# Attention in front of an expert layer: queries' transfers, grouping of weights and block sums rearranged

## The chip, the cores and the metric

The kernel runs on one core of a Trainium2 chip. The metric is device time in microseconds (us) of one execution; three timed runs of the kernel before gave 818.00, 818.36 and 817.81, median 818.0. The core's engines are TensorE (PE; PEld is its weight load), VectorE (DVE), ScalarE (ACT), GpSimd (POOL) and SyncE (SP), which here issues nearly all transfers. Each engine works through its own list of instructions in order and waits on semaphores for the others.

## The reference

```python
batch, n_heads, seq, head_dim = (4, 8, 576, 64)
scores = scale * np.matmul(q, k.transpose(0, 1, 3, 2))
log_f = np.log(np.clip(f, 0.0001, 1.0))
cum = np.cumsum(log_f, axis=-1)
decay = cum[:, :, :, None] - cum[:, :, None, :]
scores = np.where(causal, -1000000000.0, scores + decay)
scores = scores - np.max(scores, axis=-1, keepdims=True)
attn = np.exp(scores)
attn = attn / (np.sum(attn, axis=-1, keepdims=True) + 1e-09)
return np.matmul(attn, v).astype(np.float32)
```

The result, reshaped to 2304 tokens of 512 features, goes through `((x @ w1) * (x @ w2)) @ w3 @ w_out` and then through a layer of eight experts, where every token takes the expert with the largest gate. The change touches attention alone.

## The kernel before

Two heads make a pair; there are 16 pairs, numbered n from 0 to 15. 576 positions are five blocks of 128 (the last has 64). What is done for a pair is cut into stages with short names; `START` gives each stage a planned time in its pair, and `order` in `attention` sorts all stages of all pairs by `START + SHIFT + 9.8 n`. The instructions are issued in that order, and each engine then keeps it. The numbers of `START` set the order only: an instruction runs as soon as its engine comes to it and what it needs is there.

A pair goes through these stages:

- `lk`, `lq`, `lv`: SP loads transposed keys, queries, and values (288, 288 and 320 KB). `ck`: two small transfers bring the decay terms (CK).
- `kh`, `qh`: ScalarE rounds keys and queries to fp32r; `kl`, `ql`: VectorE makes the remainders. `qd` (`last_queries`): SP copies the last 64 queries of both heads from `qh` into the diagonal of a tile QD, two transfers.
- `X1`, `X3`, `X2` (with block 0) and `XL` (the last 64 queries of both heads, with QD): TensorE makes rounded scores; `m1`, `m3`, `m2`, `m0`, `mL`: VectorE takes their row maxima into M.
- `Tm`: TensorE turns the maxima (a product with the identity) into a corner of a bank; `tc`: ScalarE copies them; `mv`: SP spreads them into the rows MR.
- `GA` to `GD`: TensorE makes the exact scores, keys as rows, in four groups of columns, three terms each; `HA` to `HD` add decay and maxima as a fourth term; `eA` to `eD`: ScalarE takes the exponential of a group into the tile PT. `BANKS` says which block's columns stand in which group, `BLOCK` where a block stands in PT.
- `a0` to `a4`: POOL zeroes the upper triangle of a diagonal block (affine select). `s1` to `s3`: POOL adds blocks 0 to 3 into `ac`.
- `p0`, `p1`, `p3`: TensorE multiplies the weights with the values; `su` (`sums`): products with a column of ones sum `ac`, the first columns of block 0, and block 4 over the keys. `xa`, `sa`: ScalarE copies the result and the sums; `zs`: SP stores the sums; `rl` to `rs` invert them once per batch.

Three banks of 1024 columns (pool `pss`) go round among the X and G stages, so a G or X product waits until the exponential or the maxima three allocations before have read theirs.

In one round TensorE runs GB, GA of pair n-2, X1 of pair n, GC, X3, X2, GD, XL of pair n, Tm of pair n-1, then p0 to p3 and su of pair n-3.

Woven in is work for later products: SP loads pieces of weights (`c0`, 512 KB), ScalarE and VectorE take them apart (`c1` on ScalarE; `c2`, `c3`, `c4` on VectorE), ScalarE rounds them (`c5`, line 505), POOL makes the residual (`c6`, line 507). In eight rounds SP also issues a zero fill of `xs` (`cr`, 771 KB), and in some the broadcast of reciprocals (`xl`, tile rb).

Of the kernel before, what the change touches and what calls it, by code (L numbers as in the profile page):

```python
# [28 lines left out]
P = 128  # L29
# [11 lines left out]
EARLY = 12  # L41
LOADS = 5

BLOCK = [(0, 192), (128, 768), (256, 1216), (384, 0), (512, 1536)]
WIDTH = 1600

BANKS = {"A": [(3, 384, S), (0, 0, 288)], "B": [(0, 288, S)], "C": [(1, 128, S)], "D": [(2, 256, S), (4, 512, S)]}

PERIOD = 9.8
START = {  # L50
# [7 lines left out]
}  # L58
SHIFT = {
    (1, "lk"): -9.0, (1, "lq"): -9.2, (2, "lk"): 1.0, (2, "lq"): 1.0, (0, "Tm"): -3.7, (0, "tc"): -3.65, (0, "mv"): -3.7,  # L60
    (15, "xa"): -3.4, (15, "sa"): -3.4, (15, "zs"): -5.9, (15, "rl"): -5.9,
}

FILL = {(0, "XL"): 8, (1, "XL"): 5}

AFTER = {
    "K4_13": 4.4, "K4_14": 4.43, "K0_15": 15.6, "K0_16": 15.61, "K0_17": 15.62, "inputs": 13.6, "scores": 13.8,
# [11 lines left out]
def attention(nc, tc, ident, xT, rz, xs, wc, q, k, v, f):  # L79
# [7 lines left out]
    with (  # L87
# [136 lines left out]
        def pairwise(*products):  # L224

            for x in products:
                for h in range(2):
                    out, a, b, start, stop = x
                    PE.matmul(out(h), a(HALF[h]), b(HALF[h]), start=start, stop=stop)  # L229
# [40 lines left out]
        def turn(s):  # L270
            n = s["n"]
            if n == B * NP - 1:
                x = pss.tile([P, 1024], F32, name=f"t_{n}", tag="s")[:, 896:]
            else:
                x = st[n + 1 if n else n]["x", 4][:, 896:]
            s["t"] = x[0:64, :P]
            PE.matmul(s["t"], Ms[s["n"] % 2], ident, start=True, stop=True)

# [8 lines left out]
        def weights(s, g, last):  # L287

            n = s["n"]
            if not last:  # L290
                s["g", g] = pss.tile([P, 1024], F32, name=f"g{g}_{n}", tag="s")
            ps = s["g", g]
            terms = [(s["kh"], s["qh"]), (s["kl"], s["qh"]), (s["kh"], s["ql"])] if not last else [(CKs[n % 3], MRs[n % 2])]
            (j, q0, q1), *more = BANKS[g]
            if j == 2:
                more, s["tail"] = [], s.get("tail", []) + terms
            for i, (a, b) in enumerate(terms):
                at = 0
                for x, (j, q0, q1) in enumerate([BANKS[g][0], *more]):
                    kc, c = slice(P * j, P * j + P), slice(at, at + q1 - q0)  # L300
                    out = lambda h: ps[:, 512 * h + c.start:512 * h + c.stop]
                    pairwise((out, lambda r: a[r, kc], lambda r: b[r, q0:q1], not last and i == x == 0, last and x == len(more)))
                    at = c.stop
            if j == 2 and last:
                tail = lambda e: lambda h: ps[64 * e:64 * e + 64, 512 * h + at:512 * h + at + SL]
                pairwise((tail(1), lambda r: z[r, :SL], lambda r: z[r, :SL], True, True))
                for i, (a, b) in enumerate(s["tail"]):
                    pairwise((tail(0), lambda r: a[r, 512:S], lambda r: b[r, 512:S], i == 0, i == len(s["tail"]) - 1))

        def expo(s, g):  # L310
            w = sum(q1 - q0 for _, q0, q1 in BANKS[g])
# [35 lines left out]

        def sums(s):

            acc = s["ac"]  # L350
            for half, c, src, start, stop in (
                (1, 0, lambda h: acc[:, h, 160:448], True, False), (0, 0, lambda h: place(s, 0, h, 0, P), True, True),
                (0, P, lambda h: acc[:, h, 0:160], True, True), (1, 224, lambda h: place(s, 4, h, 512, S), False, True),
            ):
                for h in range(2):
                    r = 64 * h + 32 * half
                    x = src(h)
                    PE.matmul(s["v"][r:r + 32, c:c + x.shape[1]], ones, x, start=start, stop=stop, tile_position=(0, r))

# [2 lines left out]
            A.activation(out=xT[:, pr, S * b:S * b + S], in_=s["v"][:, 384:960], func=ACTF.Copy)  # L362

        def keep_sums(s):
            A.activation(out=tl(s, "zs", (288,)), in_=s["v"][:, 0:288], func=ACTF.Copy)

        def store_sums(s):
            b, pr = divmod(s["n"], NP)
            SP.dma_start(out=zd[pr, :, S * b:S * b + S].rearrange("h (i c) -> h i c", i=2), in_=s["zs"][0:P:32])

        def invert(s, step, late=False):

# [947 lines left out]
```

## Time and profile before

| | us |
|---|---|
| median of three timed runs | 818.0 |
| the profiled execution | 816.79 |
| its span | 815.2 |
| TensorE busy in the span | 780.6 (96%) |
| VectorE, POOL, ScalarE busy | 453.3, 320.7, 281.0 |

The span runs from the first instruction to the last. Attention takes about its first 208 us. In the page's forty slices (20.4 us each) TensorE is 0.8 or 0.9 busy in the first ten, 0.9 after that:

```profile
PE   8899888899999999999999999999999999999995
DVE  7897877785689960441333223046577836445520
POOL 5568877799100040131023021014355443445521
PEclk9899998999999999999999999999999999999999
DMA  2546566534454310100010010034576656557460
```

Each digit is a tenth of the slice (PEclk: of TensorE's full clock). A busy TensorE can still be at the lower clock. A timeline row reads: start, duration, engine, line, operation, output and inputs, shapes, count; in brackets the idle time before it and who ended it. A wait for several semaphores is put down to the one that came last by the profile.

### The profile page before, as it was taken

Reading aid. Unit: us, or ns where it says so; the run is one execution under the profiler, and the core shown is the slowest. Engines: PE = TensorE matmul, PEld = TensorE weight load, DVE = VectorE, ACT = ScalarE, POOL = GpSimd, SP = SyncE. Lnnn points to the kernel's source line nnn. Section 1 sums busy time; section 2 is a strip of 40 time slices with the busy share of each in tenths; the row PEclk is TensorE's granted clock in tenths of the full one; section 3 lists DMA queues with packets and bytes.
Section 4 is the critical chain, followed back from the end, with each engine's and each line's share of the span. In section 5 each row is a group of like instructions: output and inputs, shape, how many; then the busy total and the mean of one; then the engine's idle time right before and its main releaser. Section 6 shows DMA issues by size and latency. Waiting matters only on the chain.

```text
span 815.2 us, 13776 instructions
## 1 busy us (share of the span) xinstructions
PE 780.6 (96%) x5166; PEld 657.5 (81%) x5167; DVE 453.3 (56%) x987; ACT 281.0 (34%) x542; POOL 320.7 (39%) x339
## 2 busy tenths in 40 slices
PE   8899888899999999999999999999999999999995
PEld 4777766686788887888788788898898999999983
DVE  7897877785689960441333223046577836445520
ACT  3555554565447522221221221222222222322221
POOL 5568877799100040131023021014355443445521
PEclk9899998999999999999999999999999999999999
DMA  2546566534454310100010010034576656557460
GB/s 94 157 147 195 166 219 195 178 127 138 128 186 155 129 41 27 52 26 28 27 39 20 8 52 0 1 117 143 191 234 196 195 191 196 169 189 225 138 265 29
DMA packets 40211, 102.12 MB, mean 125 GB/s; under 512 B 8610, under 2 KB 9314, under 8 KB 39888
## 3 DMA queue, kind: packets, MB, share of 16 engines
q1 hardware_dynamic: 36960, 91.46, 35.3%
q0 software_dynamic: 3184, 9.77, 3.2%
q8 instruction: 41, 0.67, 0.3%
q14 instruction: 26, 0.21, 0.1%
HBM read 84.47 MB, written 16.51 MB: 124 GB/s over the span
## 4 chain that ended last, share of the span: by engine, by line
PE 77%; DMA 7%; POOL 6%; DVE 3%; issue 3%; SPq 2%; ACT 1%; POOLq 0%; DVEq 0%; ACTq 0%
PE a L592 4%; PE b L592 4%; PE y L594 4%; PE y L592 4%; PE a L594 4%; PE b L594 4%; PE y L593 4%; PE a L593 4%; PE b L593 4%; PE h L592 3%; PE h L594 3%; PE h L593 3%; DMA QD<-qh 3%; DMA out<-ot,id 3%; PE v L342 3%
## 5 line engine op out<-in xcount | busy, mean ns | idle before, releaser
L622 DVE TENSOR_TENSOR ga<-b,ga 128x512 f32<-128x512 f32 (+1 forms) x40 | 25.4, 636 | 144.0 <-PE b L594 143.3
L753 POOL DMA_INDIRECT xs<-xr,pos x18 | 19.0, 1055 | 172.7 <-DVE pos L747 126.6
L264 DVE CUSTOM_DVE_ANT_0 junk<-x,tri 128x256 f32<-128x256 f32 (+3 forms) x128 | 62.7, 490 | 16.9 <-PE x L229 9.6
L592 PE MATMUL h<-gh,ah 128*128 128x320 f32 (+4 forms) x224 | 67.2, 300 | 0.0
L593 PE MATMUL h<-gl,ah 128*128 128x320 f32 (+4 forms) x224 | 66.9, 299 | 0.0
L594 PE MATMUL h<-gh,al 128*128 128x320 f32 (+4 forms) x224 | 66.9, 299 | 0.0
L321 POOL TENSOR_SCALAR_AFFINE_SELECT PT<-PT 128x256 f32<-128x256 f32 (+1 forms) x80 | 55.9, 732 | 15.9 <-ACT PT L315 12.4
L592 PE MATMUL b<-xh,w2h 128*128 128x512 f32 (+1 forms) x160 | 59.9, 375 | 0.0
L592 PE MATMUL a<-xh,w1h 128*128 128x512 f32 (+1 forms) x160 | 59.8, 374 | 0.0
L594 PE MATMUL a<-xh,w1l 128*128 128x512 f32 (+1 forms) x160 | 58.9, 368 | 0.0
L594 PE MATMUL b<-xh,w2l 128*128 128x512 f32 (+1 forms) x160 | 58.9, 368 | 0.0
L593 PE MATMUL a<-xl,w1h 128*128 128x512 f32 (+1 forms) x160 | 58.8, 368 | 0.0
L593 PE MATMUL b<-xl,w2h 128*128 128x512 f32 (+1 forms) x160 | 58.8, 368 | 0.0
L342 PE MATMUL v<-PT,vr 128*64 128x448 f32 (+4 forms) x384 | 56.9, 436 | 1.5 <-POOL ac L333 1.5
L592 PE MATMUL y<-raw,gh 128*128 128x512 f32 x144 | 56.9, 395 | 0.0
L594 PE MATMUL y<-raw,gl 128*128 128x512 f32 x144 | 56.2, 390 | 0.0
L593 PE MATMUL y<-raw,gh 128*128 128x512 f32 x144 | 56.0, 389 | 0.0
L585 POOL TENSOR_SCALAR bh<-rb 128x1024 fp32r<-128x1024 f32 x28 | 37.6, 1344 | 44.1 <-DMA rb<-e 39.8
L624 ACT ACTIVATE gh<-ga 128x512 fp32r<-128x512 f32 (+1 forms) x40 | 23.5, 588 | 88.9 <-DVE ga L622 88.9
L342 PEld LDWEIGHTS v<-PT,vr 128*64 128x64 f32 x384 | 41.7, 151 | 15.4 <-issue 4.2
L1046 DVE SCALAR_TENSOR_TENSOR hl<-h,hh 128x320 fp32r<-128x320 f32 (+4 forms) x56 | 25.5, 463 | 46.9 <-ACT hh L1045 46.2
L608 POOL TENSOR_TENSOR xT<-xT,rz 128x512 f32<-128x512 f32 (+1 forms) x16 | 19.8, 1235 | 77.0 <-DMA rz<-rz 77.0
(619 smaller groups left out, 2156.0 us busy)
## 6 DMA issues: line engine op xcount, KB each, us to landing
ra<-e SPq DMA_DIRECT2D x28, 512.0 KB
rb<-e SPq DMA_DIRECT2D x28, 512.0 KB
w<-w3t SPq DMA_DIRECT2D x16, 512.0 KB
xs<-zero SPq DMA_DIRECT2D x8, 771.0 KB
vr<-v SPq DMA_DIRECT2D x16, 320.0 KB
kr<-k SPq DMA_DIRECT2D x16, 288.0 KB
qr<-q SPq DMA_DIRECT2D x16, 288.0 KB
wo<-wo SPq DMA_DIRECT2D x8, 512.0 KB
```

The costliest lines, as they stand in the source:

```text
L264: V.tensor_tensor_reduce(out=junk[:, :w], in0=s["x", i][:, 512 * h:512 * h + w] if i < 4 else s["x", i][:, 224:224 + S], in1=tri[:, 640 - ...
L321: G.affine_select(out=t, in_=t, pattern=[[0, 2], [1, w]], compare_op=ALU.is_ge, fill=0.0, base=0, channel_multiplier=-1,)
L342: PE.matmul(s["v"][HALF[h], 384 + q0:384 + q1], s["vr"][:, j, HALF[h]], place(s, j, h, q0, q1), start=(j == 0), stop=(j == 4 or q1 == P),)
L585: G.tensor_scalar(out=hi, in0=src, scalar1=1.0, scalar2=1.0, op0=ALU.mult, op1=ALU.mult)
L592: PE.matmul(ps, ah, bh, start=start and i == 0, stop=False)
L593: PE.matmul(ps, ah, bl, start=False, stop=False)
L594: PE.matmul(ps, al, bh, start=False, stop=stop and i == last)
L608: G.tensor_tensor(out=xv, in0=xv, in1=d, op=ALU.mult)
L622: V.tensor_tensor(out=ga[:, :w], in0=pb[:, :w], in1=ga[:, :w], op=ALU.mult)
L624: A.activation(out=gh[:, f, :w], in_=ga[:, :w], func=ACTF.Copy)
L753: return G.indirect_dma_start(out=xs[:, :], out_offset=bass.IndirectOffsetOnAxis(ap=pos[:, c:c + 1], axis=0), in_=rows[c], in_offset=None, ...
L1046: V.scalar_tensor_tensor(out=hl[:, f, :w], in0=ps[:, :w], scalar=0.0, in1=hh[:, f, :w].bitcast(F32), op0=ALU.max, op1=ALU.subtract)
```

## The change

Six things, in the order of the diff:

- Groups of columns: A is 288 columns of block 0, B its other 288, C block 1 with block 4 (448 and 64), D block 2 with block 3 (320 and 192); before A had block 3 with the first 288 of block 0, B 288, C block 1, D block 2 and the tail (block 4) on half the rows. A now comes before B. Products of block 4 have all 128 rows, and the zero product for the unused rows is gone.
- `qd` stands before `c0`, so ahead of the weights' load, the zero fill and the broadcasts.
- `c5` stands between `eB` and `eC` instead of after `tc`; `c6` and the selects move earlier, with a4 before a2 and a3.
- `s3` is gone: POOL adds blocks 0 to 2 only, and TensorE sums block 3's 192 columns in `sums`. The sums are split at column 384 instead of 288; they are copied in two pieces and stored with two transfers.
- Pair 1's turn (`Tm`, `tc`, `mv`) comes 4.4 of the plan's units sooner; it then uses its own pair's bank.
- Four fill products stand after X1 of pair 1.

```diff
-BLOCK = [(0, 192), (128, 768), (256, 1216), (384, 0), (512, 1536)]
+BLOCK = [(0, 0), (128, 576), (256, 1088), (384, 1408), (512, 1024)]
-BANKS = {"A": [(3, 384, S), (0, 0, 288)], "B": [(0, 288, S)], "C": [(1, 128, S)], "D": [(2, 256, S), (4, 512, S)]}
+BANKS = {"A": [(0, 0, 288)], "B": [(0, 288, S)], "C": [(1, 128, S), (4, 512, S)], "D": [(2, 256, S), (3, 384, S)]}
+HALVES = (0, 384, S)
...
-    "lk": -18.7, "lq": -18.2, "ck": -15.75, "kh": -14.1, "qh": -13.2, "c0": -12.6, "qd": -10.7,
+    "lk": -18.7, "lq": -18.2, "ck": -15.75, "kh": -14.1, "qh": -13.2, "qd": -12.5, "c0": -12.4,
...
+    (1, "Tm"): -4.45, (1, "tc"): -4.45, (1, "mv"): -4.4,
...
-FILL = {(0, "XL"): 8, (1, "XL"): 5}
+FILL = {(0, "XL"): 8, (1, "X1"): 4, (1, "XL"): 5}
...
-                x = st[n + 1 if n else n]["x", 4][:, 896:]
+                x = st[n + 1 if n > 1 else n]["x", 4][:, 896:]
...
-            (j, q0, q1), *more = BANKS[g]
-            if j == 2:
-                more, s["tail"] = [], s.get("tail", []) + terms
...
-            if j == 2 and last:
-                tail = lambda e: lambda h: ps[64 * e:64 * e + 64, 512 * h + at:512 * h + at + SL]
-                pairwise((tail(1), lambda r: z[r, :SL], lambda r: z[r, :SL], True, True))
-                for i, (a, b) in enumerate(s["tail"]):
-                    pairwise((tail(0), lambda r: a[r, 512:S], lambda r: b[r, 512:S], i == 0, i == len(s["tail"]) - 1))
...
-            acc = s["ac"]
-            for half, c, src, start, stop in (
-                (1, 0, lambda h: acc[:, h, 160:448], True, False), (0, 0, lambda h: place(s, 0, h, 0, P), True, True),
-                (0, P, lambda h: acc[:, h, 0:160], True, True), (1, 224, lambda h: place(s, 4, h, 512, S), False, True),
+            acc = lambda q0, q1: lambda h: s["ac"][:, h, q0 - P:q1 - P]
+            mid = HALVES[1]
+            for half, q0, src, start, stop in (
+                (1, mid, acc(mid, S), True, False), (0, 0, lambda h: place(s, 0, h, 0, P), True, True),
+                (1, 384, lambda h: place(s, 3, h, 384, S), False, False), (0, P, acc(P, mid), True, True),
+                (1, 512, lambda h: place(s, 4, h, 512, S), False, True),
             ):
                 for h in range(2):
-                    r = 64 * h + 32 * half
+                    r, c = 64 * half + 32 * h, q0 - HALVES[half]
...
-            A.activation(out=tl(s, "zs", (288,)), in_=s["v"][:, 0:288], func=ACTF.Copy)
+            zs, n = tl(s, "zs", (HALVES[1],)), S - HALVES[1]
+            A.activation(out=zs[:, :n], in_=s["v"][:, :n], func=ACTF.Copy)
+            A.activation(out=zs[0:64, n:], in_=s["v"][0:64, n:HALVES[1]], func=ACTF.Copy)
...
-            SP.dma_start(out=zd[pr, :, S * b:S * b + S].rearrange("h (i c) -> h i c", i=2), in_=s["zs"][0:P:32])
+            for i, (q0, q1) in enumerate(zip(HALVES, HALVES[1:])):
+                SP.dma_start(out=zd[pr, :, S * b + q0:S * b + q1], in_=s["zs"][64 * i:64 * i + 64:32, :q1 - q0])
```

The rest of `START` is told by what stands in each engine's list. On SP, in the round of pair 6, before (MR: maxima of pair 4; zd: sums; wo: a piece of weights; xs: zero fill; kr, qr: the loads for pair 7):

```order
L195 DMA MR_111<-mt_868 2x1x64
L369 DMA zd<-zs_842 2x2x288
L489 DMA wo_895<-wo 128x512
L404 DMA xs<-zero 128x3x514
L195 DMA QD_120<-qh_887 64x64 x2
L200 DMA vr_948<-v 128x640
L200 DMA kr_967<-k 128x576
L200 DMA qr_971<-q 128x576
L209 DMA CK_109<-EKd 2x576 x2
```

And now:

```order
L198 DMA MR_111<-mt_870 2x1x64
L369 DMA zd<-zs_851 2x384
L369 DMA zd<-zs_851 2x192
L198 DMA QD_120<-qh_889 64x64 x2
L489 DMA wo_904<-wo 128x512
L404 DMA xs<-zero 128x3x514
L203 DMA vr_943<-v 128x640
L203 DMA kr_969<-k 128x576
L203 DMA qr_975<-q 128x576
L212 DMA CK_109<-EKd 2x576 x2
```

QD went ahead of the weights and the zero fill; the store of the sums became two.

On ScalarE, a round in the middle, before (PT: exponentials; zs: sums; mt: turned maxima; cw: rounded weights):

```order
L315 ACTIVATE PT_941<-gB_914 128x2x288
L315 ACTIVATE PT_941<-gA_927 128x2x480
L315 ACTIVATE PT_941<-gC_958 128x2x448
L362 ACTIVATE xT<-v_870 128x576
L365 ACTIVATE zs_999<-v_870 128x288
L315 ACTIVATE PT_941<-gD_991 128x2x384
L280 ACTIVATE mt_1025<-xl_1016 9x128
L505 ACTIVATE cw<-wo1u 128x512
L215 ACTIVATE kh_116<-kr_967 128x576
L215 ACTIVATE qh_1044<-qr_971 128x576
L496 ACTIVATE w01u<-w_739 128x512
```

And now:

```order
L310 ACTIVATE PT_938<-gA_921 128x2x288
L310 ACTIVATE PT_938<-gB_931 128x2x288
L505 ACTIVATE cw<-wo1u 128x512
L310 ACTIVATE PT_938<-gC_953 128x2x512
L359 ACTIVATE xT<-v_872 128x576
L363 ACTIVATE zs_1009<-v_872 128x192
L364 ACTIVATE zs_1009<-v_872 64x192
L310 ACTIVATE PT_938<-gD_995 128x2x512
L283 ACTIVATE mt_1028<-xl_1019 9x128
L218 ACTIVATE kh_116<-kr_969 128x576
L218 ACTIVATE qh_1047<-qr_975 128x576
L496 ACTIVATE w01u<-w_747 128x512
```

The rounding of the piece wo1 went from behind the turned maxima to between the second and the third exponential.

On POOL, the same round, before (ac: the running sum; cw: the residual of the piece), from the residual on:

```order
L507 TENSOR_TENSOR cw<-wo1u,cw 128x512
L321 AFFINE_SELECT PT_941<-PT_941 128x2x128 x4
L321 AFFINE_SELECT PT_941<-PT_941 128x2x64
L333 TENSOR_TENSOR ac_1120<-PT_941 128x896
L333 TENSOR_TENSOR ac_1120<-ac_1120,PT_941 128x2x320
L333 TENSOR_TENSOR ac_1120<-ac_1120,PT_941 128x2x192
```

And now:

```order
L507 TENSOR_TENSOR cw<-wo1u,cw 128x512
L316 AFFINE_SELECT PT_938<-PT_938 128x2x128 x2
L316 AFFINE_SELECT PT_938<-PT_938 128x2x64
L316 AFFINE_SELECT PT_938<-PT_938 128x2x128 x2
L328 TENSOR_TENSOR ac_1104<-PT_938 128x896
L328 TENSOR_TENSOR ac_1104<-ac_1104,PT_938 128x2x320
```

The third add is gone and the select of the last block comes third. The order of residual, selects and adds stays; what the residual waits for stands earlier on ScalarE.

## Rows read from the trace of the kernel before

**Rows 1.** Windows of core 0: us, busy time (count) of each engine, clock, DMA share, GB/s

```profile
29.80:36.60 6.80, 6.00 (x44) 5.84 (x44) 4.48 (x9) 2.68 (x4) 4.21 (x5) 0.50 0.69 218
200.00:210.00 10.00, 8.24 (x67) 5.53 (x61) 2.93 (x5) 2.40 (x7) 7.51 (x7) 1.00 0.16 55
210.00:220.00 10.00, 10.00 (x46) 8.26 (x45) 9.70 (x18) 5.87 (x12) 0.00 (x0) 1.00 0.56 165
```

**Rows 2.** Waits of TensorE, 0 to 210 us: total, times, longest

```profile
PE xl L256 <- DMA QD<-qh: 10.4, 5, 3.3
PE xl L256 <- DVE M L264: 2.8, 3, 1.7
PE gB L229 <- DMA MR<-mt: 1.9, 1, 1.9
...
PE v L358 <- POOL ac L333: 1.8, 1, 1.8
PE v L342 <- POOL ac L333: 1.5, 2, 0.9
```

**Rows 3.** Timeline, first product of XL, pairs 3, 4, 5, 6 and 15

```profile
37.83 0.40 PE L256 MATMUL xl<-kh,QD 128*128 128x288 f32 x1
49.55 0.40 PE L256 MATMUL xl<-kh,QD 128*128 128x288 f32 x1
59.32 0.40 PE L256 MATMUL xl<-kh,QD 128*128 128x288 f32 x1
70.98 0.58 PE L256 MATMUL xl<-kh,QD 128*128 128x288 f32 x1 [1.73 <-DVE M L264]
...
179.24 0.40 PE L256 MATMUL xl<-kh,QD 128*128 128x288 f32 x1
```

**Rows 4.** Timeline of SP: issues of weights and QD in two rounds

```profile
62.71 0.36 SPq L489 DMA_DIRECT2D wo<-wo  x1
...
63.70 2.50 SPq L195 DMA_DIRECT2D QD<-qh  x2
...
75.12 0.36 SPq L489 DMA_DIRECT2D w<-w3t  x1
...
149.80 0.40 SPq L489 DMA_DIRECT2D w<-w3t  x1
```

**Rows 5.** Windows at the end of two bursts; last two columns DMA share, GB/s

```profile
71.00:72.00 1.00, 1.00 (x4) 0.93 (x4) 0.00 (x0) 0.00 (x0) 0.38 (x1) 0.50 0.45 166
...
159.50:160.00 0.50, 0.50 (x4) 0.38 (x2) 0.35 (x1) 0.50 (x2) 0.00 (x0) 0.51 0.23 74
```

**Rows 6.** Timeline of POOL and VectorE: kl alone, and in the round from 37.83

```profile
15.26 0.75 DVE L222 TENSOR_TENSOR kl<-kr,kh 128x576 fp32r<-128x576 f32 x1
...
39.47 2.11 POOL L333 TENSOR_TENSOR ac<-PT 128x896 f32<-128x896 f32 x1
40.08 2.11 DVE L222 TENSOR_TENSOR kl<-kr,kh 128x576 fp32r<-128x576 f32 x1
42.11 2.11 DVE L222 TENSOR_TENSOR ql<-qr,qh 128x576 fp32r<-128x576 f32 x1
44.14 1.24 DVE L498 TENSOR_SCALAR wo0u<-wo0u 128x512 int32<-128x512 int32 x1
```

**Rows 7.** The same two engines in the round from 59.32

```profile
61.51 1.29 POOL L507 TENSOR_TENSOR cw<-w00u,cw 128x512 fp32r<-128x512 f32 x1
61.94 1.48 DVE L222 TENSOR_TENSOR kl<-kr,kh 128x576 fp32r<-128x576 f32 x1
66.58 2.12 POOL L333 TENSOR_TENSOR ac<-PT 128x896 f32<-128x896 f32 x1
```

**Rows 8.** Groups by form, 0 to 200: count, busy us, mean ns, idle before

```profile
L333 POOL TENSOR_TENSOR ac<-ac,PT 128x384 f32<-128x384 f32 x15 | 16.2, 1079 | 1.2
L315 ACT ACTIVATE PT<-gC 128x896 f32<-128x896 f32 x16 | 14.7, 919 | 2.2 <-PE gC L229 1.3
L215 ACT ACTIVATE qh<-qr 128x576 fp32r<-128x576 f32 x16 | 10.7, 670 | 0.9 <-DMA qr<-q 0.9
L358 PE MATMUL v<-ac,ones 128*32 128x160 f32 x60 | 6.6, 299 | 0.0
```

More of the change, by code (lines that the diff above doesn't have):

```diff
@@ L293, in weights @@
             terms = [(s["kh"], s["qh"]), (s["kl"], s["qh"]), (s["kh"], s["ql"])] if not last else [(CKs[n % 3], MRs[n % 2])]
-            (j, q0, q1), *more = BANKS[g]
-            if j == 2:
-                more, s["tail"] = [], s.get("tail", []) + terms
             for i, (a, b) in enumerate(terms):
                 at = 0
-                for x, (j, q0, q1) in enumerate([BANKS[g][0], *more]):
+                for x, (j, q0, q1) in enumerate(BANKS[g]):
                     kc, c = slice(P * j, P * j + P), slice(at, at + q1 - q0)
                     out = lambda h: ps[:, 512 * h + c.start:512 * h + c.stop]
-                    pairwise((out, lambda r: a[r, kc], lambda r: b[r, q0:q1], not last and i == x == 0, last and x == len(more)))
+                    pairwise((out, lambda r: a[r, kc], lambda r: b[r, q0:q1], not last and i == x == 0, last and x == len(BANKS[g]) - 1))
                     at = c.stop
-            if j == 2 and last:
-                tail = lambda e: lambda h: ps[64 * e:64 * e + 64, 512 * h + at:512 * h + at + SL]
-                pairwise((tail(1), lambda r: z[r, :SL], lambda r: z[r, :SL], True, True))
-                for i, (a, b) in enumerate(s["tail"]):
-                    pairwise((tail(0), lambda r: a[r, 512:S], lambda r: b[r, 512:S], i == 0, i == len(s["tail"]) - 1))
         def expo(s, g):
```

8 rows, old and new, of the table START are left out of this document.

## The prediction

> **What bounds the kernel now.** I read the page's busy line and windows first, then TensorE's waits, then the timeline of the places named there. From 210 us on TensorE is busy throughout; in the ten before that for 8.24 [rows 1]. So the change, which touches only attention, has to win its time before 208 us, and what it wins is then carried through some 600 us of full TensorE.
>
> Attention runs in rounds, one pair of heads per round; I count them by the start of XL (the score product of the last 64 queries): 49.55 for pair 4, 59.32 for pair 5, 179.24 for pair 15 [rows 3]. The round from pair 4 to 5 takes 9.77. The eleven rounds from pair 4 to 15 take 129.69, 11.79 each: two microseconds a round are stalls. The largest wait by name is XL's for QD, 10.4 in five waits; the second name, VectorE's M, may hide more of the same, as a wait for several semaphores is put down to the last. At the end of attention TensorE waits 1.5 + 1.8 = 3.3 for POOL's running sum, and early once 1.9 for MR [rows 2].
>
> Why QD is late: SP issues 0.5 MB of weights at 62.71, the 771 KB zero fill, and only then QD at 63.70 [rows 4]. XL of that pair starts at 70.98 [rows 3], when the traffic is nearly over: from 71 to 72 the DMA engines are 0.45 busy [rows 5]. SP gets to the next weights at 75.12 [rows 4], since MR stands before them and waits for the turn behind XL. The DMA engines are thus idle from about 71.5 to 75.
>
> **The change part by part.**
>
> *QD ahead of weights and zero fill.* XL's wait for QD goes. What is late next? QD waits for qh, qh for the load of its queries, and that load is the last of the previous round's burst. Behind QD on SP now stand the weights, the zero fill, the broadcasts and the loads of values, keys and queries. So a loop of transfers closes: weights issued, burst lands, qh, QD issued, next weights. The burst runs from 62.71 to about 71.5 in traffic [rows 4, 5]; its last piece lands, I estimate, 9.2 after the weights' issue (8.8 to 9.6). Less 0.35 for the QD no longer in it (an estimate: 32 KB in short rows), plus 0.7 for qh [rows 8], plus 1.1 for two QD issues (the two before took 2.50 with the queue full, an issue alone about 0.5) and 0.1 of waking: 10.8 to 11.1 a round. A round with the broadcast of reciprocals issues its weights at 149.80 and ends its traffic at about 160, 10.2 later [rows 4, 5]; the same sum gives 12.2, and as I see traffic only to half a microsecond I take 12.4. Three rounds are of that kind. The second store of the sums adds one SP issue of 0.5, beside TensorE.
>
> *POOL's third add goes, its order moves.* The add of 128x384 costs 1.08 a round [rows 8]. At the end of attention POOL was the last to finish; there its 3.3 of waits go, and I take 3.0 (1 to 4), because MR of the last pair is next.
>
> In the rounds the move is worth less, perhaps nothing. POOL and VectorE take turns: in the round from 37.83 the first add runs from 39.47 to 41.58; kl starts at 40.08 and takes 2.11, where alone it took 0.75; ql takes 2.11 and the first weight step 1.24 [rows 6]. That round, in which TensorE waits for no transfer, took 49.55 - 37.83 = 11.72 [rows 3]. From the next round on ScalarE's weight rounding stands after the turn, and POOL's residual behind it, at 61.51; the add then falls at 66.58, kl takes only 1.48 [rows 7], and the round from 49.55 takes 9.77. The change puts the rounding between the second and the third exponential. POOL's residual is then early, the selects follow the exponentials, and the add starts some 2 us after D, where the round of 37.83 had it.
>
> So I price the new round by that one. From XL at 37.83: kl ends at 42.19, ql at 44.22 [rows 6]. The first weight step takes 0.62 rather than 1.24, as the third add beside it is gone; two more of 0.7: 46.2. Rounding 0.65 (a 128x576 copy is 0.67 [rows 8]): it is now in front of the third exponential, and while it waits for VectorE's last step, that exponential, the copies of the finished pair and the fourth are queued behind it, and D's product for its bank. Third exponential 0.92 [rows 8], 1.0 with 1024 instead of 896 elements; D's product 1.0 (as for the fourth block 320 and 192 columns a head in four terms); XL at 48.9. That is 11.1, and 0.2 more, since D's exponential grows from 768 to 1024 elements and moves the add. Round: 11.3. Bounds: 9.8, if the add falls beside the maxima as now, and 12.6, if POOL's residual of 1.29 [rows 7] blocks VectorE as well.
>
> [...]
>
> *TensorE's own work.* The tail products of D (ten of 64 columns) become eight in C; 192 columns move from A to D; sums gets 192 more columns a head in fp32. The nearest row, 160 columns of sums, is 0.30 an instruction, several side by side [rows 8]: I put sums at +0.2 and the tail at -0.3, so -0.1 a round (-0.4 to +0.3), hidden where the round is 11.3. The second copy of the sums on ScalarE adds some 0.3, hidden in its idle time before the fourth exponential.
>
> *Second pair's turn sooner.* In the third round B's product waits 1.9 for MR [rows 2], and TensorE's granted clock is 0.50 from 29.8 to 36.6 [rows 1], the lower of its two levels. Now the turn stands before the third pair's scores. MR is issued some microseconds sooner, but behind weights and values (0.8 MB, at the burst's 2.2 MB in 8.8 some 3.3 us), so I let it land 1.9 sooner than now, and the third pair's keys and queries, which moved behind it, only about when they are wanted. XL of pair 3 then 2.2 sooner, and the next round without the third add 0.8 shorter: -3.0 up to pair 4 (-5 if the half clock goes too, -1 if the transfers behind MR decide). The four fill products stand where TensorE waits for the first turn anyway and cost nothing; without that cover some 0.9.
>
> *Sum.* Eight rounds of 11.3 and three of 12.4 are 127.6, against 129.7: -2.1. With -3.0 before and -3.0 behind: -8.1. The profiled execution took 816.79 (span 815.2 and 1.6 around it), 1.2 below the median of 818.0; 816.8 - 8.1 = 808.7, or 809.9 beside the median. I predict 810.
>
> **Rivals.**
>
> A, *the add falls beside the maxima all the same*: then only the loop of transfers counts. For it: POOL worked that way in most rounds [rows 7]; against it: nothing in the new order holds POOL back. Five rounds of 10.9, three of 12.4, three without zero fill of 9.8 are 121; with late landings 124. So -6 to -9 in the middle and -6 outside: about 805. If the loop were shorter too, eleven rounds of 9.7 would give -23, some 790; I see no reason for that.
>
> B, *slower: rounding and residual close the loop tighter.* The rounding waits for VectorE's last weight step in front of the third exponential; the residual of 1.29 behind it can catch VectorE's next step with two operands. Round 11.3 + 1.3 = 12.6; eleven are 138.6, +8.9; with -6 outside +2.9: 821. It decides from a round of 12.3 ((129.7 + 6.0) / 11). For it: kl lost 0.73 to just that residual [rows 6, 7]; against it: the residual moves away from kl, towards the maxima.
>
> C, *the ends don't give what they should*: MR of pair 1 waits behind the weights, and at the end MR of pair 15 takes POOL's place. Then -2 in the middle and -1 outside: 815.
>
> **How the numbers follow.** Forecast 0.45, A 0.25, B 0.14, C 0.16. No change is what lies within 0.2% of 818, or 1.6 us. Of the forecast (804 to 815 by its own terms) and of A all is faster, of C about half, of B a tenth or less: 0.45 + 0.25 + 0.08 = 0.78. Within 0.2%: the other half of C and a fifth of B, 0.11; slower: the rest of B, 0.11. The range takes in A's late half and B's near edge: 802 to 820.
>
> **What would show it.** Right: no wait of XL for QD; kl and ql near 2 us in the middle rounds with an add beside each; rounds of about 11.3, and 12.4 with a broadcast; no wait for POOL's sum at the end; XL of pair 4 near 46.5. A: kl and ql below 1.6, rounds below 11, the load of queries as the last wait before the next scores. B: rounds above 12, with ScalarE waiting for VectorE in front of the rounding. C: XL of pair 4 later than 48, or TensorE idle before the last pair's first product. I would be wrong altogether if the end of attention moved and the end of the kernel didn't: then the stage behind is held by something else than TensorE.

## The result: slower, where faster was forecast

Six runs of the changed kernel gave a median of 821.95 us (820.57 to 822.54), six of the kernel before on the same chip 817.9 (814.66 to 818.36): a ratio of 1.0055, 95% interval 1.0036 to 1.0074. The forecast was 810, in a range of 802 to 820. The profiled execution has a span of 820.6 (before 815.2).

The first product of XL in the kernel after, for pairs 3, 4, 8 to 14 and 15, to be read against [rows 3]:

```profile
36.79 0.40 PE L259 MATMUL xl<-kh,QD 128*128 128x288 f32 x1
48.67 0.40 PE L259 MATMUL xl<-kh,QD 128*128 128x288 f32 x1
94.11 0.40 PE L259 MATMUL xl<-kh,QD 128*128 128x288 f32 x1
107.64 0.40 PE L259 MATMUL xl<-kh,QD 128*128 128x288 f32 x1
119.64 0.40 PE L259 MATMUL xl<-kh,QD 128*128 128x288 f32 x1
131.06 0.40 PE L259 MATMUL xl<-kh,QD 128*128 128x288 f32 x1
144.86 0.40 PE L259 MATMUL xl<-kh,QD 128*128 128x288 f32 x1
159.62 0.40 PE L259 MATMUL xl<-kh,QD 128*128 128x288 f32 x1
173.85 0.61 PE L259 MATMUL xl<-kh,QD 128*128 128x288 f32 x1
185.18 0.40 PE L259 MATMUL xl<-kh,QD 128*128 128x288 f32 x1
```

Before, pairs 8 to 14:

```profile
94.41 0.37 PE L256 MATMUL xl<-kh,QD 128*128 128x288 f32 x1 [1.46 <-DMA QD<-qh]
107.88 0.37 PE L256 MATMUL xl<-kh,QD 128*128 128x288 f32 x1 [2.14 <-DMA QD<-qh]
119.74 0.38 PE L256 MATMUL xl<-kh,QD 128*128 128x288 f32 x1 [0.56 <-DVE M L264]
132.86 0.58 PE L256 MATMUL xl<-kh,QD 128*128 128x288 f32 x1 [3.31 <-DMA QD<-qh]
145.47 0.40 PE L256 MATMUL xl<-kh,QD 128*128 128x288 f32 x1
158.12 0.38 PE L256 MATMUL xl<-kh,QD 128*128 128x288 f32 x1 [2.54 <-DMA QD<-qh]
169.47 0.40 PE L256 MATMUL xl<-kh,QD 128*128 128x288 f32 x1
```

Up to pair 4 the kernel is 0.9 ahead of before. The eleven rounds from there to pair 15 take 185.18 - 48.67 = 136.5, where before took 129.7 and the forecast had 127.6. From XL of pair 15 to the last product of the sums it takes 28.2 (before 29.3), and what follows, 607.2, is what it was (606.7). So the loss is in the eleven rounds. In four of them it can be seen at once: 13.5 from pair 8, 13.8 from pair 11, 14.8 from pair 12, 14.2 from pair 13.

The waits of TensorE, 0 to 215 us (what for: total, times, longest), against [rows 2]:

```profile
PE x L232 <- DVE M L267: 10.4, 10, 1.7
PE v L337 <- issue: 4.0, 2, 2.6
PE x L232 <- ACT qh L218: 2.5, 3, 1.2
PE gA L232 <- DMA MR<-mt: 2.2, 1, 2.2
PE v L337 <- POOL PT L316: 1.8, 2, 1.0
```

XL's wait for QD is gone, as forecast, and so is the wait for POOL's sum at the end. In their place TensorE waits for the maxima (10.4, as much as QD's wait was), for rounded queries, and in the round from pair 11 for MR; the 4.0 marked "issue" stand in the rounds from pairs 8 and 12. The round from 60.0, without a transfer late, on VectorE, ScalarE and POOL, against [rows 6, 7]:

```profile
62.00 2.10 POOL L328 TENSOR_TENSOR ac<-PT 128x896 f32<-128x896 f32 x1
62.38 2.33 DVE L225 TENSOR_TENSOR kl<-kr,kh 128x576 fp32r<-128x576 f32 x1
64.18 1.96 POOL L328 TENSOR_TENSOR ac<-ac,PT 128x640 f32<-128x640 f32 x1
64.64 2.12 DVE L225 TENSOR_TENSOR ql<-qr,qh 128x576 fp32r<-128x576 f32 x1
66.68 0.41 DVE L498 TENSOR_SCALAR wo1u<-wo1u 128x512 int32<-128x512 int32 x1
68.58 0.63 ACT L505 ACTIVATE cw<-wo1u 128x512 fp32r<-128x512 f32 x1 [1.77 <-DVE wo1u L502]
69.29 1.29 POOL L507 TENSOR_TENSOR cw<-wo1u,cw 128x512 fp32r<-128x512 f32 x1 [3.15 <-ACT cw L505]
```

This is the forecast's round: an add beside kl and one beside ql, the rounding waiting for VectorE in front of the third exponential, the residual away from kl. Six of the eleven rounds are like it and take 11.3 to 11.4; together they take 68.2, and took 67.8 before, where they were stalls and short rounds mixed. Nearly the whole loss stands in the other five, which hold a load of the sums (pairs 8 and 12) or a broadcast (9, 11 and 13): 28.3 for 26.1, and 40.0 for 35.8. ScalarE waits there for transfers, in the rounds from pairs 8, 11 and 12:

```profile
95.35 0.23 ACT L382 ACTIVATE z<-z 128x36 f32<-128x36 f32 x1 [2.50 <-DMA z<-zd]
137.40 0.68 ACT L218 ACTIVATE kh<-kr 128x576 fp32r<-128x576 f32 x1 [4.83 <-DMA kr<-k]
147.35 0.23 ACT L382 ACTIVATE z<-z 128x36 f32<-128x36 f32 x1 [3.76 <-DMA z<-zd]
```

The loop of transfers can be read from SP, from one issue of the weights to the next. In the round from pair 11, which has a broadcast:

```profile
126.94 0.53 SPq L489 DMA_DIRECT2D w<-w3t  x1
140.10 0.53 SPq L489 DMA_DIRECT2D w<-w3t  x1
```

That is 13.2. The other two loops with a broadcast take 13.2 and 14.0, the two with a load of the sums 14.0 and 13.8, and three others with a zero fill 11.0, 11.3 and 11.8.

### The profile page after: what moved, and what is told of

It reads as the page before. It is cut to its first block, busy times and chain, and to the rows that moved or that the text cites. A ratio compares the mean times of both kernels' runs of the same rounds, so it can differ in the third digit from the quotient of the medians.

```text
span 820.6 us, 13859 instructions
## 1 busy us (share of the span) xinstructions
PE 780.2 (95%) x5203; PEld 657.4 (80%) x5203; DVE 473.3 (58%) x987; ACT 282.7 (34%) x558; POOL 285.7 (35%) x323
## 5 line engine op out<-in xcount | busy, mean ns | idle before, releaser
L753 POOL DMA_INDIRECT xs<-xr,pos x18 | 19.3, 1070 | 173.4 <-DVE pos L747 126.6
L267 DVE CUSTOM_DVE_ANT_0 junk<-x,tri 128x256 f32<-128x256 f32 (+3 forms) x128 | 62.7, 490 | 10.5 <-POOL MR L136 1.9
L337 PE MATMUL v<-PT,vr 128*64 128x448 f32 (+4 forms) x384 | 51.1, 404 | 5.8 <-issue 4.0
L337 PEld LDWEIGHTS v<-PT,vr 128*64 128x64 f32 x384 | 37.1, 140 | 18.9 <-issue 9.5
L1046 DVE SCALAR_TENSOR_TENSOR hl<-h,hh 128x320 fp32r<-128x320 f32 (+4 forms) x56 | 25.4, 463 | 46.6 <-ACT hh L1045 45.9
L586 DVE TENSOR_TENSOR bl<-rb,bh 128x1024 fp32r<-128x1024 f32 x28 | 35.6, 1290 | 16.2 <-POOL bh L585 16.2
```

The source lines that it names most:

```text
L267: V.tensor_tensor_reduce(out=junk[:, :w], in0=s["x", i][:, 512 * h:512 * h + w] if i < 4 else s["x", i][:, 224:224 + S], in1=tri[:, 640 - ...
L337: PE.matmul(s["v"][HALF[h], 384 + q0:384 + q1], s["vr"][:, j, HALF[h]], place(s, j, h, q0, q1), start=(j == 0), stop=(j == 4 or q1 == P),)
L586: lo_eng.tensor_tensor(out=lo, in0=src, in1=hi.bitcast(F32), op=ALU.subtract)
L753: return G.indirect_dma_start(out=xs[:, :], out_offset=bass.IndirectOffsetOnAxis(ap=pos[:, c:c + 1], axis=0), in_=rows[c], in_offset=None, ...
L1046: V.scalar_tensor_tensor(out=hl[:, f, :w], in0=ps[:, :w], scalar=0.0, in1=hh[:, f, :w].bitcast(F32), op0=ALU.max, op1=ALU.subtract)
```

## Experiments

Each time is a median of five to eight timed runs, beside runs of the kernel before on the same chip (medians of 817.0 to 817.2); ratios are against these, with their 95% intervals. "Eleven rounds" is from XL of pair 4 to XL of pair 15 in the profile: before 129.7, after 136.5. It comes from one profiled execution, and that can lie some 2 us from its kernel's median (the last experiment's took 798.48, its four other runs 795.87 to 796.66), so differences of 1 or 2 us in it show nothing by themselves.

### The two moves, one at a time

The rounding late again in the changed kernel:

```diff
-"c5": 10.6, ... "c6": 13.9, "a1": 15.4, ... "s1": 19.6, "s2": 21.9,
+"c5": 14.6, ... "c6": 15.5, "a1": 17.1, ... "s1": 20.2, "s2": 22.5,
```

> The changed kernel with c5, c6, the selects and the two adds back at the plan's times of before (c5 14.6, c6 15.5, first add 20.2). Theory T1 (the earlier rounding puts POOL's adds beside kl and ql, and that makes the rounds long): kl near 1.5 to 1.8 and ql near 1 again, the eleven rounds from XL of pair 4 to XL of pair 15 fall from 136.5 to 124 to 130 us, kernel 808 to 815. Rival T2 (the loop of transfers, with what stands behind the burst in SP's list - MR, the load of the sums, the keys - sets the long rounds, and POOL's place is without effect): the eleven rounds stay at 134 to 138, the rounds of 13.5 to 14.7 stay where they are, kernel 820 to 823. Rival T3 (more of TensorE's work by the new groups and sums): also 820 to 823, but with TensorE's waits shorter and its busy time in the rounds longer.

Measured: 825.96, ratio 1.0097 (1.007 to 1.0124), eleven rounds 140.5. kl came down to 1.5 to 1.8 and ql to 0.95, and the rounds did not follow: they alternate, 10.1, 15.0, 11.5, 12.5, 16.2, 10.3, 14.7. T1, as the whole cause, fell here, and T2 and T3 gave less than was measured too. In the long rounds the weight steps c2 to c4 now meet POOL's adds: in the round of 15.0 c3 takes 2.48 and c4 1.90, where the round before has 0.69 and 0.77.

The same move alone, in the kernel before:

```diff
-"c5": 14.6, "c6": 15.5, "a1": 17.1, ... "s1": 20.2, "s2": 22.5, "s3": 24.1,
+"c5": 10.6, "c6": 13.9, "a1": 15.4, ... "s1": 19.6, "s2": 21.9, "s3": 23.5,
```

> The kernel before with the move of c5, c6, selects and adds alone (c5 10.6, c6 13.9, first add 19.6, second 21.9, third 23.5). T1: kl and ql near 2.1 in most rounds, the eleven rounds lengthen from 129.7 to 134 to 142, kernel 822 to 830 (the third add, which is still there, lengthens the first weight step too). T2: rounds as before, 129 to 131, kernel 817 to 819.

Measured: 822.85, ratio 1.0072 (1.0044 to 1.01), eleven rounds 136.6, none under 11.7. The early rounding lengthens the rounds, as T1 has it; TensorE's wait for QD falls to 0.5, since by the time it comes to XL QD has landed.

QD ahead of the weights alone, in the kernel before:

```diff
-"c0": -12.6, "qd": -10.7,
+"c0": -12.4, "qd": -12.5,
```

> The kernel before with QD ahead of the weights' load alone. T1: the wait of XL for QD (10.4 in five) goes and little takes its place, eleven rounds 124 to 129, kernel 812 to 817. T2: the loop of transfers closes, rounds with a broadcast or a load of the sums become 13 to 14.7, eleven rounds 133 to 138, kernel 820 to 825.

Measured: 828.67, ratio 1.0139 (1.0111 to 1.0167), eleven rounds 145.2: the largest loss of any part, past what T2 gave it. From pair 7 on, rounds of 16 to 17 alternate with rounds of 11 to 13. One of the long ones, from 81.8, in the timeline:

```profile
86.19 0.69 ACT L215 ACTIVATE kh<-kr 128x576 fp32r<-128x576 f32 x1 [2.32 <-DMA kr<-k]
87.59 1.15 SPq L195 DMA_DIRECT2D QD<-qh  x2
87.91 2.13 POOL L333 TENSOR_TENSOR ac<-PT 128x896 f32<-128x896 f32 x1
88.23 2.09 DVE L498 TENSOR_SCALAR wo2u<-wo2u 128x512 int32<-128x512 int32 x1 [1.52 <-ACT wo2u L496]
90.36 1.91 DVE L500 SCALAR_TENSOR_TENSOR wo2u<-wo,wo2u 128x512 int32<-128x512 int32 x1
92.30 1.37 DVE L502 SCALAR_TENSOR_TENSOR wo2u<-wo,wo2u 128x512 int32<-128x512 int32 x1
94.53 0.79 PE L229 MATMUL x<-kh,qh 64*128 64x384 f32 x4 [4.06 <-DVE M L264]
```

The keys come 2.3 late; so the weight's first step c1 is late, and VectorE's c2 to c4 with it. They now fall beside POOL's adds and take 2.09, 1.91 and 1.37, where other rounds of this kernel show 0.62, 0.77 and 0.77: 3.2 lost. The maxima of X1 stand behind them in VectorE's list, and the next scores wait 4.06 for these. QD is there long before it is wanted.

The weights ahead of QD again, in the changed kernel:

```diff
-"qd": -12.5, "c0": -12.4,
+"qd": -10.7, "c0": -12.6,
```

> The changed kernel with the weights' load ahead of QD again. T1: XL's wait for QD returns, but the long kl and ql stay: eleven rounds 134 to 138, kernel 819 to 824. T2: the four rounds of 13.5 to 14.7 fall to 11.5 to 12.5, eleven rounds 127 to 131, kernel 812 to 817.

Measured: 822.51, ratio 1.007 (1.0046 to 1.0093), eleven rounds 133.4, TensorE's wait for QD back at 10.0 in seven. As T1 said, except that the rounds fell a little below its range. In the time it is no different from the changed kernel.

### Neither move, and QD on another queue

Both moves undone, so that the groups, the sums on TensorE and the second pair's turn stay:

```diff
+both edits of the first and the fourth experiment
```

> The changed kernel with both moves taken back: c5, c6, selects and adds at the plan's times of before, and the weights' load ahead of QD. What stays of the change: the new groups, block 3 summed by TensorE, the second pair's turn sooner, the fills. Theory T4 (each of the two moves alone lengthens the middle, as the runs with one of them showed: eleven rounds 133.4 to 145.2 against 129.7; the rest is harmless there and worth about 1 us at the end): eleven rounds 126 to 131, the tail from XL of pair 15 to the last sums 28.2, kernel 812 to 817. Rival T3 (the new groups and the sums on TensorE lengthen the rounds): eleven rounds 133 to 138, kernel 819 to 824.

Measured: 821.8, ratio 1.0057 (1.0039 to 1.0076), eleven rounds 135.3. T4 took the rest for harmless: wrong. The numbers are those of T3. XL waits 14.1 for QD instead of 10.4.

QD issued by ScalarE behind qh, in the kernel before:

```diff
-"qd": -10.7,
+"qd": -13.1,
-move(QDs[s["n"] % 2][HALF[h], HALF[h]], s["qh"][HALF[h], 512:S])
+A.dma_start(out=QDs[s["n"] % 2][HALF[h], HALF[h]].bitcast(F32), in_=s["qh"][HALF[h], 512:S].bitcast(F32))
```

> The kernel before with QD's two transfers issued by ScalarE behind qh, so that QD is early and nothing in SP's list waits for qh. T4 with a loop through SP's list (weights, zero fill and loads stand behind QD, which waits for qh, which waits for the loads before): XL's waits for QD (10.4) go, the loads come no later than before, eleven rounds 119 to 127, kernel 807 to 815. Rival T6 (an early QD lengthens the rounds by itself, since the scores then come so early that the weight steps c2 to c4 meet POOL's adds): rounds of 15 to 16.5 as with QD ahead on SP, eleven rounds 136 to 146, kernel 822 to 830. Rival T7 (the two issues hold ScalarE for some 1.2 us a round, which eats the gain): 128 to 131, kernel 815 to 819.

Measured: 831.17, ratio 1.0179 (1.0151 to 1.0206), eleven rounds 142.3, long rounds of 15.6, 16.8 and 16.4 with m1 12 us behind XL. T6: in these three rounds c2 to c4 meet the adds (2.38, 1.91 and 1.37 in the round of 15.6). The wait for QD isn't lost time to be won; without it TensorE runs one or two rounds of 10.6 to 11.8, the loads fall behind, and the next round pays.

The same in the changed kernel without its moves:

```diff
+the edits of the last two
```

> The changed kernel with c5, c6, selects and adds at the plan's times of before, the weights' load first on SP, and QD issued by ScalarE. T4: the gains of the two runs beside it add up, eleven rounds 118 to 126, tail 28.2, kernel 804 to 812. T6: eleven rounds 134 to 144, kernel 819 to 828. T7: 126 to 130, kernel 811 to 816.

Measured: 825.91, ratio 1.0117 (1.0085 to 1.0149), eleven rounds 137.2: T6 again.

The step on the loaded sums later, in the changed kernel:

```diff
-"ra": 41.4, "rv": 42.75,
+"ra": 43.8, "rv": 44.2,
```

> The changed kernel with ra (ScalarE's step on the loaded sums) 2.4 of the plan's units later, behind the turned maxima, and rv 1.45 later. If ScalarE's wait for the sums' load (2.5 and 3.8 us in two rounds) is what makes these rounds long: the rounds from pair 8 and from pair 12 fall from 13.5 and 14.7 to 11.5 to 12.5 each, kernel 817 to 819. If these rounds are long by the loads behind the burst anyway (keys and MR next): 13 to 14.5, kernel 821 to 823.

Measured: 821.52, ratio 1.0056 (1.004 to 1.0073). The two rounds fell to 11.4 and 11.6, as expected; the rounds with a broadcast rose to 12.4, 14.4 and 15.5, the tail from 28.2 to 30.4, and the time stayed. ScalarE's wait for keys rose from 17.0 in seven to 21.1 in eight. The two rounds gave 5.3 and the rounds with a broadcast took 2.3 of it back; the eleven rounds came to 133.4, 3.1 less than in the changed kernel. The tail took 2.2, with ScalarE waiting 3.4 and 2.3 for loads of weights there. XL of pair 4 stood at 50.2, not 48.7, though nothing before it was changed: here TensorE's granted clock was 0.50 from 24.1 to 30.9, and in the changed kernel's profile it was 1.00 from 17 to 50.

### Fewer transfers in the rounds

The eight zero fills, 6.2 MB, moved out of the rounds to about 283 us, in the kernel before; no work is left out:

```diff
-SP.dma_start(out=xs[e * N:e * N + W]..., in_=st["zt"]...)        # in clear_rows
+for e in range(E): SP.dma_start(out=xs[e * N:e * N + W]..., in_=zt...)   # behind the load of the gates
```

> The kernel before with the eight zero fills of xs (771 KB each) taken out of the rounds and issued after attention, at about 290 us, when the DMA engines are idle. Theory T8 (the rounds of before are paced by the transfers: QD lands behind weights and fill, and the wait for it sets eleven of them): without the fill the rounds fall towards 9.8, what the two rounds without a fill took, eleven rounds 108 to 116 against 129.7, kernel 797 to 806. Rival (the other loads pace as much): 122 to 128, kernel 811 to 816.

Measured: 797.55 (795.72 to 799.74), ratio 0.9757 (0.9733 to 0.978), eleven rounds 111.6, each of 9.7 to 10.6 after the first. TensorE's waits from 48 to 160 are one line:

```profile
PE x L229 <- DVE M L264: 1.7, 3, 0.6
```

The same in the changed kernel:

> The changed kernel with the same move of the fills. Theory T9 (its floor of 11.4 us a round is VectorE behind POOL's adds, and only what lies above 11.4 comes from transfers): all rounds 11.3 to 11.8, eleven rounds 124 to 128 against 136.5, kernel 808 to 813, slower than the kernel before with the same move. If the transfers alone set the rounds: eleven rounds 108 to 116, kernel 797 to 806, the same as the kernel before with the move.

Measured: 813.46, ratio 0.995 (0.9929 to 0.9971), eleven rounds 126.6, rounds of 11.3 to 12.0. With the fills out of the way the change costs 126.6 - 111.6 = 15.0 us in the rounds and 15.9 in the time.

And with POOL's two adds left out; the running sum is filled with ones in their place:

```diff
-G.tensor_tensor(out=acc[:, :, q0 - P:], in0=..., in1=src, op=ALU.add)
+if j == 1: G.memset(acc, 1.0)
```

> The changed kernel with the fills moved and POOL's two adds left out: the running sum is filled with ones instead, so the softmax denominators and what is routed by them are not the reference's; only the rounds of attention are read from it. T9: kl and ql at 0.75 to 1.0 with nothing of POOL beside them, rounds 9.6 to 10.3, eleven rounds 106 to 113. Rival (the floor of 11.4 comes from ScalarE's rounding, which waits in front of the third exponential, or from TensorE's products): rounds stay 11.2 to 11.6, eleven rounds 123 to 128.

Measured in one profile: eleven rounds 115.0, the six without a broadcast or a load of the sums 10.06 each. A round of it:

```profile
67.96 0.85 POOL L329 MEMSET ac<- 128x896 f32 x1
68.51 0.75 DVE L225 TENSOR_TENSOR kl<-kr,kh 128x576 fp32r<-128x576 f32 x1
69.18 0.75 DVE L225 TENSOR_TENSOR ql<-qr,qh 128x576 fp32r<-128x576 f32 x1
72.69 0.63 ACT L502 ACTIVATE cw<-w01u 128x512 fp32r<-128x512 f32 x1
```

So of the 11.35 of such a round, 1.3 are VectorE held up by the adds. ScalarE's early rounding, still in its place, is not what makes the floor: the next kernel has it late and takes 10.06 too.

The changed kernel without its two moves, the fills moved:

> The changed kernel without its two moves (rounding late, weights' load ahead of QD) and with the fills moved: new groups, block 3 summed by TensorE, second pair's turn sooner. T8 and T9: rounds 9.9 to 10.3, as its rounds without a fill were (10.0 and 10.1), eleven rounds 110 to 116, end of attention 1 us sooner by the tail, kernel 797 to 806. If the added products on TensorE cost more than they give: 1 to 3 us slower than the kernel before with the same move.

Measured: 798.96, ratio 0.9772 (0.9749 to 0.9795), eleven rounds 112.9. Against 797.55 this is no clear difference; the rounds are 10.1 instead of 9.8, the tail is 28.2 instead of 29.4. So of the 15.0 the two moves together cost 126.6 - 112.9 = 13.7 and the rest of the change 1.3.

### What was still open

The stores of the sums behind the values, in the changed kernel without its two moves (fills in the rounds):

```diff
-"zs": 35.9,
+"zs": 38.85,
```

> The changed kernel without its two moves (fills back in the rounds), with the two stores of the sums on SP behind the weights, fill and values instead of in front of the weights. If the second store's issue lengthens the loop of transfers (last maxima, MR, stores, weights, fill, QD, last maxima), which is what made the rounds of this kernel 0.5 longer each than those of before: eleven rounds 124 to 130 against 135.3, kernel 812 to 817. If the loop is longer for another reason (the sums' products or the groups on TensorE): 133 to 137, kernel 820 to 823.

Measured: 812.17, ratio 0.9959 (0.9937 to 0.998), eleven rounds 125.4. SP in one round, without this edit and with it:

```profile
74.65 1.20 SPq L198 DMA_DIRECT2D MR<-mt  x2
75.91 1.01 SPq L369 DMA_DIRECT2D zd<-zs  x2
77.02 0.36 SPq L489 DMA_DIRECT2D w<-w3t  x1
```

```profile
70.09 1.16 SPq L198 DMA_DIRECT2D MR<-mt  x2
71.35 0.36 SPq L489 DMA_DIRECT2D w<-w3t  x1
```

From MR to the weights it is 2.37 with the stores between and 1.26 without. That 1.1 a round came back as 9.9 in eleven, unevenly: the two rounds with a load of the sums grew by 0.8 each, the rounds from pairs 5 and 6 gave 2.3 and 2.9. The edit takes away both stores, while the change had added only the second. In the kernel before, with one store, MR to the weights took 1.85; so the second adds 0.5 a round, as much as this kernel's rounds are longer (135.3 for 129.7). It was not taken away alone.

QD ahead of the weights, fills moved, otherwise the kernel before:

> The kernel before with QD ahead of the weights and the fills after attention. If QD ahead did harm only because the transfers behind it then came too late (keys, and through them the weight steps and the maxima): rounds 9.8 to 10.6 as without that move, eleven rounds 110 to 114 against 111.6, kernel 796 to 800. If the order on SP harms by itself: rounds of 12 to 16 remain, eleven rounds 122 to 145, kernel 809 or more.

Measured: 808.88 (804.64 to 811.82), ratio 0.9908 (0.9877 to 0.9939). Neither expectation holds: the profiled execution took 806.1, and nine of its eleven rounds take 9.8 to 11.3, as without the move, but one took 16.6 and the next 11.6, eleven rounds 120.1. In the long one ScalarE waited 3.0 for the keys, and c2 to c4 met the adds, as above. ScalarE's step on the sums waited 2.7 in that round too. Even with fewer bytes, what stands behind QD on SP is late now and then, and once was enough for 8.5.

The second pair's turn sooner alone, fills moved, otherwise the kernel before:

```diff
+(1, "Tm"): -4.45, (1, "tc"): -4.45, (1, "mv"): -4.4,
-FILL = {(0, "XL"): 8, (1, "XL"): 5}
+FILL = {(0, "XL"): 8, (1, "X1"): 4, (1, "XL"): 5}
```

> The kernel before with the fills after attention and, of the change, the second pair's turn sooner with its four fill products. My forecast put 2.2 on this turn: XL of pair 4 at 45.5 to 46.5 instead of 48.2, kernel 795 to 796.5. If the transfers behind the turn decide (as in the changed kernel, 0.9): XL of pair 4 at 47 to 48, kernel 796.5 to 798. With four more fill products in the way: 48.2 to 49, kernel 797.5 to 799.

Measured: 796.53 (795.87 to 798.48), ratio 0.9753 (0.9732 to 0.9773), XL of pair 3 at 36.7 (36.5 without), of pair 4 at 49.7 (48.2). No gain that can be told; the profiled execution was the slowest of the five, so its 49.7 is no sign of a loss either. Of TensorE's waits from 17 to 50 one changed: without the turn's move 1.4 for MR, with it 1.5 for the rounded queries. MR, issued 3.5 sooner, now stands ahead of the third pair's keys and queries; ScalarE gets to these about one later (kh at 29.98, before 29.04), and the wait only changes its name.

## Why the prediction was wrong

Of the sum's three terms, -3.0, -2.1 and -3.0, the runs gave -0.9, +6.8 and -1.0. The step that decides is the middle one, "Eight rounds of 11.3 and three of 12.4 are 127.6, against 129.7": it held the stalls of before for removed and the loop of transfers for hidden beside 11.3, gave the broadcasts too little and the loads of the sums nothing, and the middle took 136.5.

**The early part, -3.0.** It gave -0.9. The wait for MR went, and in this profile the clock of 0.50 too (1.00 from 17 to 50, where before it was 0.50 from 29.8 to 36.6), for which the forecast allowed even -5. XL of pair 2 came 0.6 later, the round from pair 2 took 1.6 less, the next 0.2 more, where 0.8 less was forecast. One step failed where it let the third pair's loads land "only about when they are wanted": the queries were the next to be late, TensorE waited 1.2 for them at 31.7, and 1.5 in the last experiment. The other failed on POOL's adds: two of them still stand beside ql and c2 in the round from 36.8, which took 11.9. With the fills moved XL of pair 4 stood at 48.1, and with the adds left out as well at 45.9. How much of the 0.9 is the change is open: the run with the step on the sums later has the same order up to there and was at 50.2.

**The rounds of 11.3.** Right in mechanism and size. Six were forecast of this kind without a broadcast or a load of the sums, and took 68.2 for 67.8. kl and ql take 2.33 and 2.12 beside an add, 0.75 each without, and kl ends 0.6 behind its add. The two adds last 2.10 and 1.96 (62.00 and 64.18), 4.06 together; beside them kl and ql took 2.95 more together, and the round 1.3; that the rest lay beside other work is argued, not shown.

What was wrong is the row that these rounds were weighed against. The forecast set 11.3 against the 11.79 that a round of before took, and called the difference a gain. But the undisturbed round of before, with the adds beside the maxima, takes 9.8, which the forecast had read too; the 11.79 are that and some 2 us that go when the fills go. So a round of the changed kernel is 1.5 longer wherever transfers don't pace: with the fills moved 11.35 against 9.8. Of this 1.3 are the adds beside kl and ql, which the move of the rounding put there, as the kernels without the adds and without the two moves both show (10.06); 0.3 are the rest of the change.

**The rounds with a broadcast, 12.4.** They took 12.0, 13.8 and 14.2: 2.8 more than the sum had. The term that was too small is the loop with a broadcast: 12.4 in the sum, 13.2, 13.2 and 14.0 from weights to weights. **The rounds with a load of the sums had no term at all** and stood at 11.3; they took 13.5 and 14.8, 5.7 more. The load stands behind weights, fill and values on SP, ScalarE's step on it in front of the exponentials that TensorE needs; taking ScalarE's step later cured these two rounds. With 0.4 of the ordinary rounds this is 8.9, the middle's whole miss.

In the rounds with only a zero fill the loop was near its price of 10.8 to 11.1 (11.0 to 11.8) and hidden, as forecast. No run shows two small terms of that price, 0.35 for QD's bytes and 0.1 of waking, nor the full queue by which the forecast explained the 2.50 of QD's two issues; measured are 2.50 behind the zero fill (63.70 before), 1.14 to 1.17 ahead of it in the changed kernel, and the loops as a whole. The second store, taken as beside TensorE, lies in the loop: 0.5 an issue between MR and what follows, and taking both stores out of it, in the kernel without the two moves, gave 9.9.

What the forecast did not have at all is what lateness does to VectorE. In the kernels with the rounding late, a late key load sends c2 to c4 into the adds, and the maxima stand behind them; with QD ahead alone lateness of 2.3 made a round of 16 where others take 10. In the changed kernel the adds lie beside kl and ql already, c2 to c4 take 0.41 to 0.69 even in its long rounds, and what makes these longer is the wait for the late transfers.

**XL's wait for QD, 10.4 in five.** The forecast took it for stall to be removed. It went, and it was pacing: TensorE waited there for transfers that the round needed anyhow. The four kernels in which QD alone was made earlier (by SP's list, by ScalarE's in two of them, with fewer bytes) were all slower than the same kernel without that. In the changed kernel itself, with its rounding early, QD's place made no difference that can be told (822.51 and 821.95).

**The tail, -3.0.** It gave -1.0. The waits for POOL's sum went; POOL's selects (1.8 in two) took their place, which wait for the late exponentials, not MR as the forecast had it.

**The rivals.** The result, 822, is where rival B was (821), not by B's mechanism: kl and ql met no residual, and the ordinary round was 11.4, below B's 12.3. C's early end came true in kind (pair 4 later than 48), its tail not by MR. That 822 lies beside B's 821 is luck. Early (2.1), middle (8.9), tail (2.0) and 0.5 in the stage behind make up the 13.5 between forecast and measured span.

**Still open.** How much each edit weighs in the full change can't be added up: one undone by itself gave nothing, both undone gave nothing, and the second store alone is seen only through taking away both. With fills in the rounds the parts replace each other; only with them moved can a part's price be read by itself. Why a loop with a broadcast takes 13.2 to 14.0 was not tested.

## What to carry over

A wait that ends on a transfer may be the pace of the whole loop of transfers: before removing it, ask which load is late next, and try the kernel with fewer bytes in the loop. Compare a forecast round with the undisturbed round of before, not with an average that has stalls of another cause in it. Here the work to move was the zero fill, not the queries: 19.5 us from transfers put where the DMA engines were little used (before, their share from 283 to 340 was 0.14, in the eleven rounds 0.61).

## What the runs showed of the hardware

On average the DMA engines were far from full where transfers set the pace (a mean share of 0.61 before, 0.53 with QD ahead alone). The windows over the eleven rounds: before, with the fills moved, the changed kernel with the fills moved, and QD ahead alone (length, busy of PE, PEld, DVE, ACT, POOL; granted clock, DMA share, GB/s):

```profile
49.60:179.20 129.60, 116.69 (x1234) 92.34 (x1232) 103.88 (x259) 74.11 (x123) 106.02 (x98) 0.92 0.61 181
```

```profile
48.20:159.90 111.70, 109.70 (x1237) 87.80 (x1233) 102.62 (x259) 74.78 (x123) 106.12 (x98) 0.98 0.49 154
```

```profile
48.06:174.67 126.61, 112.88 (x1256) 92.05 (x1254) 118.53 (x259) 74.82 (x134) 77.45 (x89) 0.99 0.42 136
```

```profile
49.74:194.90 145.16, 125.53 (x1235) 99.49 (x1233) 113.08 (x257) 74.47 (x123) 103.63 (x99) 0.85 0.53 162
```

The rounds of the kernel before, with 0.61 at 181 GB/s, were yet paced by transfers, as each burst waited for an issue that waited for the one before: from 62.7 to 71.5 the share was 0.88 at 256 GB/s, from 72 to 74 it was 0.00.

The granted clock went with the stalls. Read in windows of 0.25 us it was 0.50 or 1.00 before, but for the windows in which it turned; in the first 215 us it was 0.50 for 30.7 us in seven spells before, 51.2 with QD ahead alone, where the rounds of 16 to 17 had waits of 3.3 to 4.8 us, 10.2 with the fills moved, and none with the changed kernel's fills moved and the adds left out. The means of these whole executions are 0.979, 0.967, 0.991 and 0.996. Five of the seven spells before begin between 0.9 us ahead of the end of one of XL's waits of 1.46 to 3.31 us and 1.4 us behind it. For the same products TensorE is busy 116.7 before, 109.7 with the fills moved and 125.5 with QD ahead alone: of the 18.1 that moving the fills won in the rounds, some 7 are busy time, at a mean clock of 0.98 instead of 0.92, and 11 idle time; of the 15.5 that QD ahead lost, some 9 are busy time, at 0.85.

A VectorE step with one tensor operand (c2, line 498) took 2.09 beside an add with QD ahead alone, and 0.41 to 0.62 with no add beside it; one with two (kl) took 2.33 beside an add, and 0.75 with none.
